# Fourier mixing and a gated feed-forward on one core: block 1 of sequence 0 takes the ordinary norm path, and four DMA issues move to later slots

## The chip, the cores and the metric

The kernel runs on one core of one Trainium2 chip. The metric is device time in microseconds (us). Before the change the median of 3 runs is 859.65 us (859.43 to 859.67).

## What is computed

Eight sequences `x[b]` of 3008 rows and 256 columns are filtered in the frequency domain along the rows, and the result goes row by row through an RMS norm and a gated feed-forward with 1536 hidden columns:

```python
X = np.fft.rfft(x, axis=1)
y = np.fft.irfft(X * (filt_r + 1j * filt_i)[None], n=x.shape[1], axis=1)
rows = y.reshape(8 * 3008, 256)
xn = rows / np.sqrt(np.mean(rows * rows, axis=-1, keepdims=True) + 1e-06) * rms_g
g = xn @ w_gate
out = (g * (1 / (1 + np.exp(-g))) * (xn @ w_val)) @ w_out
```

## The kernel before

**The Fourier part of a sequence.** 3008 is 47 x 64, and the transforms are matrix products in two steps. A sequence is read in four chunks (`x_load`, L174, issued on POOL's DMA queue into four buffers; 384 KB as it lands). `a_unit` (L213) does the first step on TensorE (PE), with one matmul of 128x512 (L204), and ACT or DVE copies the result from the matmul banks to the tile t1 (L195 or L197); there are 12 such units in a sequence, three for each chunk. When a chunk is done, `z_store` (L216) writes it to a buffer in DRAM on SP's DMA queue, and `t2_load` (L226) reads it back in another order once all four stores have landed. `b_unit` (L243, matmuls in L248) does the second step and multiplies by the filter; `bi_unit` (L287) and then `n_unit` (L313) do the inverse steps, with DMA transpositions (`yt_load` L280, `t4_load` L303) between them. The first steps of sequence 0 have functions of their own and fill the first 43 us.

**The norm and the feed-forward.** A sequence is handled in 6 blocks of 512 rows. For each block a normed and transposed tile xn is made, and then 12 items use it, one for each 128 hidden columns (`gv`, L539): four matmuls of 128x512 (L553, into the banks pg and pv), the silu on ACT (L557) and the product on DVE (L558). Two items later `down` (L561) multiplies by the last weights (L578). There are 8 x 6 x 12 = 576 items, and PE runs them in order. The banks pg and pv exist twice each, so item i needs those of item i - 2 to be read.

The ordinary way to xn, used for all blocks but two, is `n_unit` (one matmul of 128x512 on PE in L321, a copy to the tile y on ACT, twice), `sq_unit` (L325: squares with sums on ACT, two instructions for each half), `stat_unit` (L332: two small instructions on POOL, L337 and L339), `xt_unit` (L342: the scaling on POOL, L347) and `tr_unit` (L352: a DMA transposition on SP's queue, L356). Block 0 of sequence 0 has `first_norm` (L445). Block 1 of sequence 0 has four functions of its own before the change, which make xn without a DMA: `n_first` (L480) makes y already transposed, by 8 matmuls of 128x128 (L489), with two squares and two copies on ACT; `q_unit` (L498) sums the squares by 8 matmuls with a column of ones (L503) and takes the power on POOL (L509); `scale_split` (L512) makes two halves of the scale on DVE; `scale_apply` (L519) spreads it over the partitions by 8 matmuls of 128x128 (L525), and two multiplications on DVE (L530) write xn.

**What sets the order.** The order of issue is planned by hand in *slots*, one for each of the 576 items. `at(slot, fn, ...)` (L749) puts a function into a slot; in the last loop (L879 on) each item issues its `gv`, then what its slot holds, then `down` of the item two before. A slot is only a place in each engine's program: an engine goes on to its next instruction as soon as the semaphores that this one waits for are there, whatever slot the other engines are in. `fit` (L756) looks for the first slot from a wished one on in which the shared matmul banks ("M" and "B") are free and the load on ACT ("A") and DVE ("V") stays under a bound; `norm_plan` (L775), `a_plan` (L784) and `b_plan` (L799) use it. `norm_plan(b, m, slots, r)` puts the two `n_unit`s at the slots given (or later), their `sq_unit`s one slot behind each, and `stat_unit`, `xt_unit` and `tr_unit` so many slots behind the second as `r` says. Before the change, block 1's four functions stand at slots 3, 5, 7 and 9, and the load tables are set by hand for them (L829 to L831). Block 1's first item is item 12.

The chunks of sequence 2 are read at the slots that `XAT[2]` gives, or two slots behind the last `a_unit` of the chunk whose buffer they take, if that is later. The four stores of sequence 1 stand at slot 2 and, in `a_plan`, one slot behind the third unit of each chunk.

Of the kernel before, what the change touches and what calls it, by code (L numbers as in the profile page):

```python
# [10 lines left out]
FP32 = mybir.dt.float32  # L11
FP16 = mybir.dt.float16
AXT = mybir.ActivationFunctionType
ALU = mybir.AluOpType
# [6 lines left out]
P = 128  # L21
D = 256
B = 8
# [9 lines left out]
Y_SCALE = N * S_INV_B * S_INV_A  # L33
XC = 6
# [67 lines left out]
def kernel(  # L102
# [11 lines left out]
    nc = tc.nc  # L114
# [17 lines left out]
    xtp = ctx.enter_context(tc.tile_pool(name="xtp", bufs=2))  # L132
    up = ctx.enter_context(tc.tile_pool(name="up", bufs=2))
    xnp = ctx.enter_context(tc.tile_pool(name="xnp", bufs=4))
    hp = ctx.enter_context(tc.tile_pool(name="hp", bufs=4))
    op = ctx.enter_context(tc.tile_pool(name="op", bufs=2))
# [4 lines left out]
    psB = ctx.enter_context(tc.tile_pool(name="psB", bufs=1, space=bass.MemoryType.PSUM))  # L141

    tab = glob.tile([P, 5 * P], FP16)
    wa, wai, ident = (tab[:, ts(i, P)] for i in range(3))
# [13 lines left out]
    ones = glob.tile([P, 1], FP16)  # L158
    epsb = glob.tile([P, 1], FP32)
    warm = glob.tile([P, 4], FP32)  # L160
    mhalf = glob.tile([P, 4], FP32)
    seen = glob.tile([P, 4], FP16)

    st = {b: {"x": {}, "t1": {}, "t2": {}, "s": {}, "yt": {}, "t4": {}, "y": {}, "sq": {},
              "u": {}, "xn": {}} for b in range(B)}
# [4 lines left out]
    def y_tile():  # L170
        t = stg.tile([P, 2, 4, 256], FP32, tag="stg", name="y")
        return t.rearrange("p a b c -> p (a b c)")[:, 0:1024].rearrange("p (a e) -> p a e", a=2)
# [16 lines left out]
    def bank(i, name):  # L189
        pool, tag = ((psM, "mx"), (psG, "pg"), (psV, "pv"), (psB, "mb"), (psO, "po0"))[i]  # L190
        return pool.tile([P, 512], FP32, tag=tag, name=name)

    def copy(eng, out, in_, scale=None):
        if eng == "A":
            nc.scalar.activation(out=out, in_=in_, func=AXT.Copy, **({} if scale is None else {"scale": scale}))  # L195
        elif scale is None:
            nc.vector.tensor_copy(out=out, in_=in_)  # L197
        else:
            nc.vector.tensor_scalar(out=out, in0=in_, scalar1=scale, scalar2=None, op0=ALU.mult)
# [277 lines left out]
        nc.scalar.activation(out=warm, in_=mhalf, func=AXT.Silu)  # L477
        st[0]["xn"][0] = xn

    def n_first(m):  # L480
        y = y_tile()
        sq = xtp.tile([P, 4, D], FP16, tag="xt", name="sq").rearrange("p (a e) d -> p a (e d)", a=2)
        psn = [bank((0, 3)[h], "psn") for h in range(2)]
        for h in range(2):
            for q in (2 * h, 2 * h + 1):
                n1p = 4 * m + q
                src = st[0]["t4"][n1p // XC][:, n1p % XC]
                for dh in range(2):
                    nc.tensor.matmul(psn[h][:, ts(2 * (q % 2) + dh, P)], src[:, ds(dh * P, P)], wai,  # L489
                                     start=True, stop=True)  # L490
        for h in range(2):
            nc.scalar.activation(out=sq[:, h, :], in_=psn[h], func=AXT.Square)
        for h in range(2):
            copy("A", y[:, h, :], psn[h])
        st[0]["sq"][m] = sq
        st[0]["y"][m] = y

    def q_unit(m):  # L498
        sq = st[0]["sq"].pop(m)
        ps = psB.tile([P, 4], FP32, tag="mb", name="psq")  # L500
        for q in range(4):
            for dh in range(2):
                nc.tensor.matmul(ps[:, q:q + 1], sq[:, q // 2, ts(2 * (q % 2) + dh, P)], ones,  # L503
                                 start=(dh == 0), stop=(dh == 1))
        u = up.tile([P, 4], FP32, tag="u", name="u")
        rho = up.tile([P, 4], FP32, tag="rho", name="rho")
        nc.vector.tensor_scalar(out=u, in0=ps, scalar1=1.0 / D, scalar2=1e-6 * Y_SCALE * Y_SCALE,
                                op0=ALU.mult, op1=ALU.add)
        nc.gpsimd.tensor_tensor(out=rho, in0=u, in1=mhalf, op=ALU.pow)  # L509
        st[0]["u"][m] = rho  # L510

    def scale_split(m):  # L512
        rho = st[0]["u"].pop(m)
        hl = up.tile([P, 2, 4], FP16, tag="hl", name="hl")
        nc.vector.tensor_copy(out=hl[:, 0, :], in_=rho)
        nc.vector.tensor_tensor(out=hl[:, 1, :], in0=rho, in1=hl[:, 0, :], op=ALU.subtract)
        st[0]["u"][m] = hl

    def scale_apply(m, bk):  # L519
        hl = st[0]["u"].pop(m)  # L520
        y = st[0]["y"].pop(m)
        ps = bank(bk, "psr")
        for q in range(4):
            for e in range(2):
                nc.tensor.matmul(ps[:, ts(q, P)], hl[:, e, q:q + 1].to_broadcast([P, P]), ident,  # L525
                                 start=(e == 0), stop=(e == 1))
        xn = xnp.tile([P, 4, 2, P], FP16, tag="xn", name="xn")
        pv = ps.rearrange("p (q t) -> p q t", q=4)
        for h in range(2):
            nc.vector.tensor_tensor(out=xn[:, 2 * h:2 * h + 2],  # L530
                                    in0=pv[:, 2 * h:2 * h + 2].unsqueeze(2).to_broadcast([P, 2, 2, P]),
                                    in1=y[:, h, :].rearrange("p (q e t) -> p q e t", q=2, e=2), op=ALU.mult)
        st[0]["xn"][m] = xn

    LAST = (B - 1, 5)
    hh_of = {}
    po_of = {}
# [92 lines left out]
    with tc.manual_schedule():  # L630
# [48 lines left out]
        todo = [(i, f, dh) for i in range(2) for f in range(2) for dh in range(2)][:7] + [(2, 0, 0)]  # L679
# [58 lines left out]
        a_out(1, 2, "V", ahead[0])  # L738

        items = [(b, m, jt) for b in range(B) for m in range(6) for jt in range(JT)]  # L740
        plan, late = {}, {}
        front = (sq_unit, s_part, add_unit)
        load = {r: [0.0] * (len(items) + 99) for r in "MBAV"}
        room = {"A": 0.8, "V": 0.7}
# [2 lines left out]
            load["V"][i] = 0.68  # L747

        def at(slot, fn, *a):  # L749
            todo = (late if fn == q_unit else plan).setdefault(slot, [])  # L750
            if fn in front:
                todo.insert(0, (fn, a))
            else:
                todo.append((fn, a))
# [20 lines left out]
        def norm_plan(b, m, slots, r):  # L775
            for i in range(2):
                s = fit(slots[i], ("M", 0, 1), ("A", 0, 0.6), ("A", 1, 0.82))
                at(s, n_unit, b, m, i)
                at(s + 1, sq_unit, b, m, i)
            for d, fn in zip(r, (stat_unit, xt_unit, tr_unit)):  # L780
                at(s + d, fn, b, m)
            assert s + r[-1] + 1 < 72 * b + 12 * m

        def a_plan(b, slots):  # L784
            for i in range(4 * (b == 1), 12):
                opts = []
                for k in "MB":
                    opts.append((k, "A", ((k, 0, 1), ("A", 0, 0.6))))
                    opts.append((k, "V", ((k, 0, 1), (k, 1, 1), ("V", 0, 0.68))))
                k, e, need = min(opts, key=lambda o: fit(slots[i], *o[2], keep=False))  # L790
                s = fit(slots[i], *need)
                at(s, a_unit, b, i, e, 0 if k == 'M' else 3)
                if i % 3 == 2:
                    at(s + 1, z_store, b, i // 3)
                    if b + 1 < B:
                        at(max(s + 2, XAT.get(b + 1, (0,) * 4)[i // 3]), x_load, b + 1, i // 3)
            return s + 1
# [20 lines left out]
                        at(last, bi_unit, b, u)  # L818
            return last

        XAT = {2: (6, 8, 11, 29), 3: (47, 51, 79, 88), 4: (112, 122, 132, 142)}
        at(0, a_out, 1, 3, "A", ahead[1])
        at(2, z_store, 1, 0)
        at(XAT[2][0], x_load, 2, 0)
        at(3, n_first, 1)
        at(5, q_unit, 1)
        at(7, scale_split, 1)
        at(9, scale_apply, 1, 3)
        load["M"][3] = load["M"][4] = 1  # L829
        load["B"][3] = load["B"][4] = load["B"][5] = load["B"][9] = load["B"][10] = 1  # L830
        load["A"][3] = load["A"][4] = 1.2  # L831
        for m, n_at in ((2, 12), (3, 20), (4, 31), (5, 42)):
            norm_plan(0, m, (n_at, n_at + 2), (2, 3, 6))
        for b in range(1, B):
            t = (b - 1) * 72
# [43 lines left out]
        for i in range(len(items) + 4):  # L879
            for fn, a in early.pop(i, ()):  # L880
                fn(*a)
            if i < len(items):
                gv(*items[i])
            for fn, a in plan.pop(i, ()):
                fn(*a)
            if 2 <= i < len(items) + 2:
                b, m, jt = items[i - 2]
                if jt == 1 and i > JT:
                    down(b, m, 0)
                if jt or i < JT:  # L890
                    down(b, m, jt)
                if items[i - 2][2] == JT - 1:
                    stores[i + 1] = items[i - 2][:2]
            for fn, a in late.pop(i, ()):
                fn(*a)
            if i in stores:
                o_store(*stores[i])
        assert not plan and not late and not early


# [28 lines left out]
```

## Time and profile before

| what | value |
|---|---|
| median of 3 runs | 859.65 us (859.43 to 859.67) |
| the profiled execution | 859.65 us |
| its span, first to last instruction | 857.9 us |
| around the span | 1.75 us |
| mean granted clock of PE | 1.000 |
| PE busy from 43 to 150 us | 107.0 of 107 us |
| DMA engines from 43 to 150 us | 82% busy, 164 GB/s |
| x loads (384 KB), issue to landing | 6.1 us (median of 31) |
| z stores, issue to landing | 2.7 us (median of 28) |
| transpositions to xn, issue to landing | 3.0 / 3.6 / 8.1 us (least, median, most of 46) |

A line of a timeline gives the start and the length of an instruction (or of several alike, with their number) in us, the engine, the line of the kernel, the operation, and what is written from what. Matmuls overlap, so the cost of one on PE is read from start to start. SPq is the DMA queue that SP issues to; a DMA's length there is the time that the issue takes, and its landing is told apart. POOL, with the name of a DMA operation, is such an issue by POOL. A page of waits names who waited, for whom, and how long. The granted clock is the share of TensorE's full clock that the chip gave.

### The profile page before, as it was taken

The page shows a single profiled execution, that of the slowest core. Times are in us where ns is not written, and L with a number is a line of the kernel's source. Part 1 is how long each engine was busy: PE and PEld are TensorE (multiplying, and loading weights), DVE is VectorE, ACT ScalarE, POOL GpSimd, SP SyncE. Part 2 cuts the span into 40 slices and gives each one's busy share as a digit, 9 for nine tenths or more (in the row PEclk, how much of TensorE's full clock was granted, in tenths as well). Part 3 has the DMA queues.
Part 4 walks back from the last instruction along what each step waited for, and adds up shares of the span by engine and source line. Part 5 has one row for each costly group of instructions (what it writes and reads, how often), then busy time and mean ns, then how long its engine had stood idle before and what let it go on. Part 6 is the DMA issues. An engine that isn't in the chain of part 4 may idle for free.

```text
span 857.9 us, 17015 instructions
## 1 busy us (share of the span) xinstructions
PE 849.2 (99%) x6139; PEld 532.5 (62%) x6139; DVE 557.2 (65%) x926; ACT 612.5 (71%) x1338; POOL 298.1 (35%) x346
## 2 busy tenths in 40 slices
PE   8999999999999999999999999999999999999997
PEld 6766666666666666666666666666666666665655
DVE  5857755776666666666666676767666665555554
ACT  4987887786687757887578865887567765777444
POOL 5725732543154413443044430444123430132000
PEclk9999999999999999999999999999999999999999
DMA  9995878756975566746747658434574431521101
GB/s 282 273 206 126 152 169 168 148 123 137 186 138 140 108 142 114 158 117 129 152 122 115 120 108 185 105 81 113 122 126 93 98 69 42 123 56 50 63 25 50
DMA packets 198237, 107.98 MB, mean 126 GB/s; under 512 B 158566, under 2 KB 182520, under 8 KB 198152
## 3 DMA queue, kind: packets, MB, share of 16 engines
q1 hardware_dynamic: 189464, 85.52, 44.9%
q0 software_dynamic: 8544, 21.24, 12.9%
q8 instruction: 48, 0.79, 0.4%
q14 instruction: 37, 0.30, 0.1%
q10 hardware_dynamic: 144, 0.13, 0.0%
HBM read 45.78 MB, written 35.65 MB: 95 GB/s over the span
## 4 chain that ended last, share of the span: by engine, by line
PE 97%; DMA 1%; DVE 0%; ACT 0%; POOL 0%; issue 0%; DVEq 0%; POOLq 0%
PE po L578 29%; PE pg L553 28%; PE pv L553 28%; PE psb L248 3%; PE psi L292 3%; PE psn L321 2%; PE psa L204 2%; DMA fs<-in_filt_i_dram 1%; PE psy L425 1%; PE psf L396 1%; PE pst L374 0%; POOL xc L186 0%; DVE s L238 0%; ACT ff L195 0%; ACT sq L455 0%
## 5 line engine op out<-in xcount | busy, mean ns | idle before, releaser
L558 DVE TENSOR_TENSOR hh<-pv,sg 128x512 f16<-128x512 f32 (+1 forms) x577 | 391.6, 679 | 283.4 <-ACT sg L557 220.5
L557 ACT ACTIVATE sg<-pg 128x512 f16<-128x512 f32 (+1 forms) x577 | 337.5, 585 | 215.2 <-PE pg L553 211.4
L553 PE MATMUL pg<-xn,wg 128*128 128x512 f16 (+2 forms) x1156 | 337.9, 374 | 0.0
L553 PE MATMUL pv<-xn,wv 128*128 128x512 f16 (+2 forms) x1156 | 337.8, 374 | 0.0
L578 PE MATMUL po<-wo,hh 128*128 128x256 f16 x2256 | 332.7, 272 | 0.0
L578 PEld LDWEIGHTS <-hh 128*128 128x128 f16 x2256 | 213.4, 98 | 105.2
L275 POOL TENSOR_TENSOR ss<-s,s 128x384 f16<-128x384 f16 x112 | 102.0, 912 | 267.4 <-DVE s L241 239.8
L553 PEld LDWEIGHTS <-wv 128*128 128x128 f16 x1156 | 113.0, 98 | 130.6 <-issue 0.2
L553 PEld LDWEIGHTS <-wg 128*128 128x128 f16 x1156 | 111.5, 98 | 16.9 <-issue 0.2
L347 POOL TENSOR_TENSOR xt<-y,rho 128x1024 f16<-128x1024 f32 (+1 forms) x46 | 85.4, 1857 | 2.9
L329 ACT ACTIVATE junk<-y 128x256 f16<-128x256 f32 x180 | 74.3, 413 | 2.8
L238 DVE TENSOR_TENSOR s<-psb,ff 128x384 f16<-128x384 f32 x124 | 67.8, 548 | 0.7 <-ACT ff L195 0.6
L241 DVE TENSOR_TENSOR s<-psb,ff 128x384 f16<-128x384 f32 x124 | 67.7, 547 | 0.0
L195 ACT ACTIVATE uu<-psi 128x384 f16<-128x384 f32 (+1 forms) x127 | 61.8, 487 | 1.1
L195 ACT ACTIVATE y<-psn 128x512 f32<-128x512 f32 (+1 forms) x95 | 55.7, 588 | 4.2
L292 PEld LDWEIGHTS <-yt 96*128 96x128 f16 x512 | 35.5, 97 | 26.2 <-issue 0.2
L339 POOL TENSOR_TENSOR rho<-u,mhalf 128x4 f32<-128x4 f32 (+1 forms) x46 | 46.5, 1011 | 3.8
L337 POOL TENSOR_SCALAR u<-ss 128x4 f32<-128x4 f32 (+1 forms) x46 | 8.9, 194 | 106.4 <-ACT junk L329 105.4
L195 ACT ACTIVATE t<-psa 128x512 f16<-128x512 f32 x70 | 41.4, 595 | 2.8 <-PE psa L204 1.4
L292 PE MATMUL psi<-wi,yt 96*128 96x96 f16 x512 | 42.9, 205 | 0.0
L248 PE MATMUL psb<-wb,t 96*128 96x96 f16 x480 | 40.0, 206 | 0.0
L248 PEld LDWEIGHTS <-t 96*128 96x128 f16 x480 | 29.3, 97 | 10.7 <-issue 0.2
(102 smaller groups left out, 364.2 us busy)
## 6 DMA issues: line engine op xcount, KB each, us to landing
out_dram<-o SPq DMA_DIRECT2D x40, 512.0 KB, 3.5
xc<-in_x_dram POOLq DMA_DIRECT2D x31, 384.0 KB, 6.1
z_tmp<-t SPq DMA_DIRECT2D x28, 384.0 KB, 2.7
t<-z_tmp SPq DMA_DIRECT2D x28, 384.0 KB, 6.0
out_dram<-o SPq DMA_DIRECT2D x7, 384.0 KB, 2.7
fs<-in_filt_i_dram POOLq DMA_DIRECT2D x3, 512.0 KB, 10.8
fs<-in_filt_r_dram POOLq DMA_DIRECT2D x3, 512.0 KB, 11.3
ws<-in_moe_w_gate_dram POOLq DMA_DIRECT2D x3, 512.0 KB, 10.0
```

Source lines behind the costliest of these rows:

```text
L195: nc.scalar.activation(out=out, in_=in_, func=AXT.Copy, **({} if scale is None else {"scale": scale}))
L238: eng.tensor_tensor(out=o, in0=ps, in1=f1, op=ALU.mult)
L241: eng.tensor_tensor(out=o, in0=ps[:, :, ::-1, :], in1=f2, op=ALU.mult)
L248: nc.tensor.matmul(ps[:, ts(k, KR)], st[b]["t2"][kk // KC][:, kk % KC, ds(dh * P, P)], wb[0:KR, kk, :], start=True, stop=True)
L275: nc.gpsimd.tensor_tensor(out=ss3[g % 3][:, :, dh, 0:KR], in0=s[0], in1=s[1], op=ALU.add)
L292: nc.tensor.matmul(ps[:, k, :], yt[0:KR, k, dh, :], wi[0:KR, 4 * g + k, :], start=True, stop=True)
L329: nc.scalar.activation(out=junk, in_=y[:, i, ts(u, D)], func=AXT.Square, accum_out=ss[:, 2 * i + u:2 * i + u + 1])
L347: nc.gpsimd.tensor_tensor(out=xt[:, 0:n, :], in0=y.rearrange("p a (u d) -> p (a u) d", u=2)[:, 0:n, :], in1=rho[:, 0:n].unsqueeze(2).to_br ...
L553: nc.tensor.matmul(ps[:, (r0 - q0) * P:(r1 - q0) * P], wt[:, dt_, ts(jt, P)], xn[:, r0:r1, dt_, :], start=(dt_ == 0), stop=(dt_ == 1))
L557: nc.scalar.activation(out=sg[:, c], in_=pg[:, 0:w], func=AXT.Silu)
L558: nc.vector.tensor_tensor(out=hh[:, c], in0=pv[:, 0:w], in1=sg[:, c], op=ALU.mult)
L578: nc.tensor.matmul(po[q - 1][:, 0, :] if own else po[q // 2][:, q % 2, :], hh_of[(b, m, j)][:, ts(q, P)], wo[:, j, :], start=(j == 0 and ( ...
```

## The change

Block 1 of sequence 0 goes the ordinary way: `norm_plan(0, 1, (2, 3), (2, 3, 5))` takes the place of its four functions, which are removed, with what the planner held for them (the dictionary `late`, and the loads set by hand). Three reads of sequence 2 (its chunks 0, 1 and 2) are put at slots 12, 13 and 15 in place of 6, 8 and 11. The store of chunk 1 of sequence 1 is put at slot 9; before, it stood one slot behind its third unit.

In the issue order of each engine this gives: on PE, one L321 matmul at slot 2 and one at slot 3 in place of the groups L489, L503 and L525, and one L204 matmul moves from slot 6 to slot 4, its copy from ACT to DVE. On ACT, two copies and four squares with sums in place of two squares and two copies. On DVE, the five small and large instructions of L507, L515, L516 and L530 go. On POOL, L337, L339 and L347 stand where L509 stood, and the three loads L186 come directly behind L347, as they came directly behind L509. On SP, one transposition L356 stands between the first and the second store L218. All other instructions keep their order.

```diff
-    def n_first(m):
...
-    def q_unit(m):
...
-    def scale_split(m):
...
-    def scale_apply(m, bk):
...
-        plan, late = {}, {}
+        plan = {}
...
         def at(slot, fn, *a):
-            todo = (late if fn == q_unit else plan).setdefault(slot, [])
+            todo = plan.setdefault(slot, [])
...
                 if i % 3 == 2:
-                    at(s + 1, z_store, b, i // 3)
+                    at(9 if (b, i) == (1, 5) else s + 1, z_store, b, i // 3)
...
-        XAT = {2: (6, 8, 11, 29), 3: (47, 51, 79, 88), 4: (112, 122, 132, 142)}
+        XAT = {2: (12, 13, 15, 29), 3: (47, 51, 79, 88), 4: (112, 122, 132, 142)}
         at(0, a_out, 1, 3, "A", ahead[1])
         at(2, z_store, 1, 0)
         at(XAT[2][0], x_load, 2, 0)
-        at(3, n_first, 1)
-        at(5, q_unit, 1)
-        at(7, scale_split, 1)
-        at(9, scale_apply, 1, 3)
-        load["M"][3] = load["M"][4] = 1
-        load["B"][3] = load["B"][4] = load["B"][5] = load["B"][9] = load["B"][10] = 1
-        load["A"][3] = load["A"][4] = 1.2
+        norm_plan(0, 1, (2, 3), (2, 3, 5))
```

More of the change, by code (lines that the diff above doesn't have):

```diff
@@ L478, in first_norm @@
         st[0]["xn"][0] = xn
-    def n_first(m):
[L481 to L496, printed above, removed]
@@ L498, in q_unit @@
-    def q_unit(m):
[L499 to L510, printed above, removed]
@@ L512, in scale_split @@
-    def scale_split(m):
[L513 to L517, printed above, removed]
-    def scale_apply(m, bk):
[L520 to L533, printed above, removed]
@@ L893 @@
                     stores[i + 1] = items[i - 2][:2]
-            for fn, a in late.pop(i, ()):
-                fn(*a)
             if i in stores:
                 o_store(*stores[i])
-        assert not plan and not late and not early
+        assert not plan and not early
 _INS = ['x', 'filt_r', 'filt_i', 'moe_w_gate', 'moe_w_val', 'moe_w_out', 'moe_rms_g']
```

## The prediction

> **What bounds the kernel now.** I read the shares of each engine, then the chain that ended last, then what TensorE (PE) waited for, all of the profile before.
>
> ```profile
> PE 849.2 (99%) x6139; PEld 532.5 (62%) x6139; DVE 557.2 (65%) x926; ACT 612.5 (71%) x1338; POOL 298.1 (35%) x346
> ...
> PE 97%; DMA 1%; DVE 0%; ACT 0%; POOL 0%; issue 0%; DVEq 0%; POOLq 0%
> ```
>
> PE is busy for 99% of the span and is 97% of the chain. Asked for PE's waits from 43 us on (where the feed-forward part begins) to the end, the profile lists none. So any PE work removed there shortens the run by its own length, and any wait that the change gives PE lengthens it by its own length, since no gap is left to take it up.
>
> The timeline of PE around the change (start, length, engine, line, operation):
>
> ```profile
> 47.30 0.61 PE L489 MATMUL psn<-tab,t 128*128 128x128 f16 x8
> 47.74 0.60 PE L578 MATMUL po<-wo,hh 128*128 128x256 f16 x4
> ...
> 51.00 0.34 PE L503 MATMUL psq<-ones,sq 128*128 128x1 f16 x8
> 51.20 0.59 PE L553 MATMUL pg<-xn,wg 128*128 128x512 f16 x2
> ...
> 56.83 0.61 PE L525 MATMUL psr<-tab,hl 128*128 128x128 f16 x8
> 57.27 0.38 PE L204 MATMUL psa<-xc,tab 128*128 128x512 f16 x1
> ...
> 60.95 0.59 PE L553 MATMUL pg<-xn,wg 128*128 128x512 f16 x2
> ...
> 61.82 0.38 PE L321 MATMUL psn<-t,tab 128*128 128x512 f16 x1
> 62.03 0.60 PE L578 MATMUL po<-wo,hh 128*128 128x256 f16 x4
> ```
>
> From start to start, the three groups of block 1's own norm cost 0.44, 0.20 and 0.44 us; an ordinary norm matmul (L321) costs 0.21. The matmul at 60.95 is the first that reads block 1's normed tile: this is the deadline of everything below.
>
> **The change, part by part.**
>
> *PE.* Removed: 0.44 + 0.20 + 0.44 = 1.08 us. Added: two L321 matmuls, 0.43. Sum **-0.65 us**, on the path. One forward-transform matmul (L204) moves from slot 6 to slot 4: no change in sum. The deadline becomes 60.95 - 0.65 = 60.30.
>
> *ACT and DVE.* ACT loses two squares and two copies of 128x512 (about 0.5 us each) and gets two copies and four squares with sums (two of them take 0.95 by the rows at 66.45 to 67.42), 0.9 us more. The silu of slot 4 then ends near 50.0 instead of 50.3, the multiplication behind it near 50.8; PE reuses their banks at 51.2 and 51.6. So nothing waits. DVE loses 1.75 us and gets a copy of 0.69. Both are hidden by the slack in the two engines (71% and 65%).
>
> *POOL and the transposition.* This is the new path to the deadline. Its pattern is block 2's in the same trace (ACT, POOL, and the DMA queue of SP):
>
> ```profile
> 67.33 0.19 ACT L329 ACTIVATION_READ_ACCUMULATOR junk<-y 128x1 f32 x1
> ...
> 67.61 0.19 POOL L337 TENSOR_SCALAR u<-ss 128x4 f32<-128x4 f32 x1 [11.04 <-ACT junk L329]
> 67.90 1.04 POOL L339 TENSOR_TENSOR rho<-u,mhalf 128x4 f32<-128x4 f32 x1
> 69.02 1.89 POOL L347 TENSOR_TENSOR xt<-y,rho 128x1024 f16<-128x1024 f32 x1
> ...
> 70.94 1.26 SPq L356 DMA_TRANSPOSE xn<-xt  x1
> ```
>
> From the last sum (67.52) to the transposition's issue it takes 3.4 us. For block 1: the two norm matmuls start at 46.0 and 47.5 (their tiles landed by 46.06, where POOL's L733 was released), the second copy ends near 48.5, and ACT then does two squares, a silu and two squares: last sum near 50.95, issue near **54.3**. A transposition that has the DMA engines for itself lands 3.0 us (that at 363.40) to 3.6 us (that at 70.94) after its issue: 57.9, 2.4 us ahead of the deadline. So far the change would be a gain of 0.65.
>
> *The x loads.* In POOL's program the three loads of sequence 2 now stand directly behind the xt multiplication. A slot orders only what one engine issues. POOL issues a load without waiting for the transposition, which SP issues when the same multiplication ends. So the loads, issued at 52.83, 53.4 and 55.98 before, go at 54.25, 54.9 and 55.8: in the same moment as the transposition, not behind its landing. That moment occurs later in this trace, with one load:
>
> ```profile
> 387.29 0.64 POOL L186 DMA_DIRECT2D xc<-in_x_dram  x1
> ...
> 387.37 1.23 SPq L356 DMA_TRANSPOSE xn<-xt  x1
> ```
>
> The load comes 0.08 us before the transposition, as at 265.63 and 265.72. Both of these transpositions landed 5.9 us after issue. DMA queues from 390.1 to 391.1 us (packets, MB, share of 16 engines; q0 is POOL's, q1 SP's):
>
> ```profile
> q1 hardware_dynamic: 62, 0.02, 12.0%
> ...
> q0 software_dynamic: 63, 0.19, 99.6%
> ```
>
> One packet of the load (3 KB) goes for one of the transposition (256 bytes). A load is 384 KB, 128 packets; a transposition is 256 KB, 1024 packets. So it creeps until the load is through, and most of its packets go behind it. Two more loads are 2 x 128 / 63 = 4.1 us more; 250 more of its packets slip through meanwhile, which saves some 0.3 at the end. Landing: 5.9 + 4.1 - 0.3 = 9.7 us after issue, at **64.0**. PE waits 64.0 + 0.05 - 60.30 = **3.75 us**. The extremes for this landing are 3.0 us (no wait) and 5.9 + 4.1 + 1.2 (a second load that starts as slowly as the one of 116.92, behind which packets were scarce for 1.2 us): a wait of 0 to 5.2. I take 9.7, since both rows nearest to it have the same issue order.
>
> [...]
>
> *The store of sequence 1* (second of four) goes behind the transposition in SP's queue: 53.10 becomes 55.6. What waits behind it are the third (its data are ready at 56.1) and the fourth store (61.34). They share SP's DMA queue with the transposition, so now their packets follow it, from about 63.3; three stores take 3 us of packets, so the last lands near 67.4. Their reader, the load L228, was issued at 66.06, landed 4.7 us later, and PE took it at 71.14: 0.38 us to spare. With PE 3.75 later, that load goes behind the output store of block 0 near 69, as far ahead of PE as before. Cost nothing, because PE's own wait covers it; without that wait it is 0 to 1.5 us (rival B).
>
> *Sum.* The profiled execution took 859.65 us (span 857.9, 1.75 around it), which is also the median. 859.65 - 0.65 + 3.75 = 862.75, so **862.8 us**. Own range 861.0 (only two loads in front: a landing after 7.9) to 864.0 (the slow start).
>
> **Rivals.**
>
> *B: the transposition gets through beside the loads, not slower.* It decides at one point, a landing less than 6.0 us after issue. For it: 5.9 with one load would just do; SP's issue could win over POOL's, or a turn hold several of its packets. Against it: the one-for-one turns, and three loads. Then PE doesn't wait at the deadline, but the transposition and the later loads push the fourth store back by up to 1.3 us, and L248's first weights come up to 1.5 us late: 859.65 - 0.65 + 0 to 1.5, that is 859.0 to 860.5; I say 860.0. Chance 0.16.
>
> *C: the wait also slows PE's clock.* At the span's start, after idleness, ten matmuls of 128x512 that cost 0.22 each later took 4.01 us, 1.7 too long:
>
> ```profile
> 1.45 4.01 PE L433 MATMUL pf<-ss 128*128 128x512 f16 x10 [1.45 <-DVE epsb L632]
> ```
>
> If PE's wait brings this back, 862.8 + 1.7 = 864.5. Against it: no idle time inside the span is as long, so none shows it, and waits to 0.64 us did nothing. [...] Chance 0.12.
>
> *D: the removed PE work is worth more than its length,* or the loads are held elsewhere and nothing is late: 859.0 or less. Chance 0.04; nothing in the profile speaks for more than 0.65.
>
> **How the numbers follow.** Forecast 0.68, C 0.12, B 0.16, D 0.04. A measurement of this kernel tells 0.2% (1.7 us) from no change. Above 861.4: the forecast and C but for a tail, 0.79. Within: B, D's greater part and that tail, 0.19. Faster: 0.02. For the range the forecast and C alone leave out a little over 0.2, so it reaches into B: 860.2 to 865.0.
>
> **What would show it.** In the profile after: a PE wait of some 3.7 us at the first pg matmul of block 1 near 60.3, put down to the DMA of xn; L186 and L356 issued within 0.2 us of each other near 54.3; that transposition landing 9 to 10 us after issue, and few of SP's packets until the loads are through. PE's sum there is right if the pg matmul is ready at 60.3. No PE wait at that matmul and one at L248 would be B; pf-like slow matmuls behind the wait, or a granted clock below 1, would be C. I am wrong if the x loads start later than the transposition lands.

## The result, and the profile after

The changed kernel takes 863.46 us (median of 6 runs, 862.65 to 865.56) against 859.61 us (6 runs, 859.43 to 859.78): a ratio of 1.005, with a 95% interval of 1.0035 to 1.0064. It is slower by about 0.45%. The runs of the kernel before lie within 0.35 us, those of the changed one within 2.9, and the granted clock sorts them: 862.65, 862.71 and 862.87 at a mean of 1.000, 864.06 at 0.998, 865.37 and 865.56 at 0.995. The profiled execution is that of 862.71 us (span 860.9).

From L498 on, a line of the changed kernel has a number lower by 55: its `gv` matmuls are L498, its `down` is L523. Shares of the engines, and the chain that ended last:

```profile
PE 849.6 (99%) x6117; PEld 532.1 (62%) x6117; DVE 555.9 (65%) x922; ACT 612.5 (71%) x1343; POOL 299.7 (35%) x348
...
PE 95%; DMA 2%; POOL 1%; ACT 1%; DVE 0%; issue 0%; POOLq 0%
```

PE's share of the chain fell from 97% to 95%, and POOL, ACT and more of the DMA now stand in it. The waits of PE from 40 to 160 us name the place (who waited, for whom, then us in total, times, and the longest):

```profile
PE pg L498 <- DMA xn<-xt: 3.5, 1, 3.5
PE psr L473 <- DVE rho L468: 0.2, 1, 0.2
```

The second is at 42.4 us, ahead of block 0's first item, and stands in the kernel before too. So from 43 us on there is one wait, and the DMA that ends it is the transposition of block 1's normed tile. On PE's timeline the two new norm matmuls, and the first matmul of block 1 (brackets at the end of a line tell how long the engine was idle before it, and what released it):

```profile
45.90 0.38 PE L321 MATMUL psn<-t,tab 128*128 128x512 f16 x1
...
47.42 0.38 PE L321 MATMUL psn<-t,tab 128*128 128x512 f16 x1
...
63.88 0.59 PE L498 MATMUL pg<-xn,wg 128*128 128x512 f16 x2 [3.52 <-DMA xn<-xt]
```

POOL's timeline, with the path to the transposition and, directly behind it, the three loads:

```profile
50.88 0.18 POOL L337 TENSOR_SCALAR u<-ss 128x4 f32<-128x4 f32 x1 [3.44 <-ACT junk L329]
51.16 1.05 POOL L339 TENSOR_TENSOR rho<-u,mhalf 128x4 f32<-128x4 f32 x1
52.28 1.89 POOL L347 TENSOR_TENSOR xt<-y,rho 128x1024 f16<-128x1024 f32 x1
54.12 1.28 POOL L186 DMA_DIRECT2D xc<-in_x_dram  x2
55.67 0.59 POOL L186 DMA_DIRECT2D xc<-in_x_dram  x1 [0.27 <-PE psa L204]
```

And SP's queue:

```profile
54.20 1.23 SPq L356 DMA_TRANSPOSE xn<-xt  x1
55.54 5.36 SPq L218 DMA_DIRECT2D z_tmp<-t  x3
68.06 0.68 SPq L546 DMA_DIRECT2D out_dram<-o  x1
68.98 2.22 SPq L228 DMA_DIRECT2D t<-z_tmp  x3
```

The first load is issued 0.08 us before the transposition. What the two queues moved from 57.25 to 58.25 us (packets, MB, share of the 16 engines):

```profile
q0 software_dynamic: 62, 0.19, 96.3%
q1 hardware_dynamic: 63, 0.02, 12.2%
```

In that 1 us, 62 packets of the loads and 63 of the transposition went, one for one, as at 390 us in the kernel before (63 and 62). The transposition, issued at 54.20, is there when PE goes on at 63.88, 9.7 us later.

### The profile page after: what moved, and what is told of

It is laid out like the page before. It is cut to its first block, busy times and chain, and to the rows that moved or that the text cites. A ratio compares the mean times of both kernels' runs of the same rounds, so it can differ in the third digit from the quotient of the medians.

```text
span 860.9 us, 16980 instructions
## 1 busy us (share of the span) xinstructions
PE 849.6 (99%) x6117; PEld 532.1 (62%) x6117; DVE 555.9 (65%) x922; ACT 612.5 (71%) x1343; POOL 299.7 (35%) x348
## 4 chain that ended last, share of the span: by engine, by line
PE 95%; DMA 2%; POOL 1%; ACT 1%; DVE 0%; issue 0%; POOLq 0%
PE po L523 28%; PE pg L498 28%; PE pv L498 28%; PE psb L248 3%; PE psi L292 3%; PE psn L321 2%; PE psa L204 2%; DMA xn<-xt 1%; DMA fs<-in_filt_i_dram 1%; PE psy L425 1%; PE psf L396 1%; PE pst L374 0%; POOL xc L186 0%; POOL xt L347 0%; DVE s L238 0%
## 5 line engine op out<-in xcount | busy, mean ns | idle before, releaser
L503 DVE TENSOR_TENSOR hh<-pv,sg 128x512 f16<-128x512 f32 (+1 forms) x577 | 391.2, 678 | 287.8 <-ACT sg L502 220.0
L498 PE MATMUL pg<-xn,wg 128*128 128x512 f16 (+2 forms) x1156 | 337.9, 374 | 3.5 <-DMA xn<-xt 3.5
L498 PE MATMUL pv<-xn,wv 128*128 128x512 f16 (+2 forms) x1156 | 337.8, 374 | 0.0
L523 PE MATMUL po<-wo,hh 128*128 128x256 f16 x2256 | 332.6, 272 | 0.0
L523 PEld LDWEIGHTS <-hh 128*128 128x128 f16 x2256 | 213.5, 98 | 105.5
L498 PEld LDWEIGHTS <-wv 128*128 128x128 f16 x1156 | 113.0, 98 | 130.7 <-issue 0.2
L498 PEld LDWEIGHTS <-wg 128*128 128x128 f16 x1156 | 111.6, 98 | 20.5 <-issue 3.9
L347 POOL TENSOR_TENSOR xt<-y,rho 128x1024 f16<-128x1024 f32 (+1 forms) x47 | 87.2, 1856 | 2.9
L339 POOL TENSOR_TENSOR rho<-u,mhalf 128x4 f32<-128x4 f32 (+1 forms) x47 | 47.5, 1011 | 3.9
L337 POOL TENSOR_SCALAR u<-ss 128x4 f32<-128x4 f32 (+1 forms) x47 | 9.1, 193 | 113.0 <-ACT junk L329 111.8
L248 PE MATMUL psb<-wb,t 96*128 96x96 f16 x480 | 40.0, 206 | 0.0
L248 PEld LDWEIGHTS <-t 96*128 96x128 f16 x480 | 29.3, 97 | 10.7 <-issue 0.2
```

What stands on the lines that cost most here:

```text
L248: nc.tensor.matmul(ps[:, ts(k, KR)], st[b]["t2"][kk // KC][:, kk % KC, ds(dh * P, P)], wb[0:KR, kk, :], start=True, stop=True)
L347: nc.gpsimd.tensor_tensor(out=xt[:, 0:n, :], in0=y.rearrange("p a (u d) -> p (a u) d", u=2)[:, 0:n, :], in1=rho[:, 0:n].unsqueeze(2).to_br ...
L498: nc.tensor.matmul(ps[:, (r0 - q0) * P:(r1 - q0) * P], wt[:, dt_, ts(jt, P)], xn[:, r0:r1, dt_, :], start=(dt_ == 0), stop=(dt_ == 1))
L503: nc.vector.tensor_tensor(out=hh[:, c], in0=pv[:, 0:w], in1=sg[:, c], op=ALU.mult)
L523: nc.tensor.matmul(po[q - 1][:, 0, :] if own else po[q // 2][:, q % 2, :], hh_of[(b, m, j)][:, ts(q, P)], wo[:, j, :], start=(j == 0 and ( ...
```

## The experiments

Ten kernels ran, all but one of them edits of the changed kernel. E8 and E9 build on e1. "Before" is the kernel before, run beside them on the same chip: 859.75 us beside e1, e3, e4 and e7, 859.68 beside e0, e2, e6 and e8, 859.72 beside e5 and e9.

| kernel | median us (runs) | range | ratio to before (95%) | granted clock of the runs |
|---|---|---|---|---|
| e0 changed kernel again | 864.35 (5) | 862.83 to 865.45 | 1.0053 (1.004 to 1.0066) | 1.000, 3 x 0.998, 0.995 |
| e1 loads behind the landing | 860.95 (11) | 860.56 to 861.80 | 1.0013 (1.0005 to 1.0022) | 0.999 to 1.000 |
| e4 one load beside | 863.44 (4) | 862.06 to 865.23 | 1.0046 (1.003 to 1.0061) | 2 x 1.000, 0.998, 0.995 |
| e5 two loads beside | 862.75 (4) | 862.17 to 863.28 | 1.0035 (1.0021 to 1.0049) | 2 x 1.000, 2 x 0.998 |
| e2 loads at the old slots | 863.77 (5) | 863.36 to 865.96 | 1.0048 (1.0034 to 1.0061) | 4 x 0.998, 0.996 |
| e6 store at the old slot | 864.49 (4) | 862.88 to 864.68 | 1.0052 (1.0038 to 1.0065) | 1.000, 3 x 0.998 |
| e3 PE busy in the wait | 863.22 (5) | 862.74 to 864.35 | 1.0042 (1.003 to 1.0055) | 0.999 to 1.000 |
| e7 wait made longer | 866.67 (5) | 866.10 to 866.79 | 1.0078 (1.0066 to 1.0091) | 4 x 0.996, 0.998 |
| e8 first load early | 860.45 (11) | 859.66 to 861.26 | 1.0008 (0.9999 to 1.0017) | 0.999 to 1.000 |
| e9 two loads early | 859.47 (11) | 859.06 to 860.56 | 0.9999 (0.999 to 1.0008) | 0.999 to 1.000 |

**Theory and rivals.** The theory is the prediction's: POOL issues the x loads in the same moment as SP issues the transposition, they share the DMA engines packet by packet, and PE waits for what comes of it. Its rivals: the new path through ACT, POOL and the DMA is too long by itself; the stores behind the transposition are what costs; and, for the spread, that either the clock or the landing differs from run to run.

**e1: the loads wait for the landing.**

```diff
+        def see(m):
+            nc.gpsimd.tensor_copy(out=seen, in_=st[0]["xn"][m][:, 0, 0, 0:4])
...
         norm_plan(0, 1, (2, 3), (2, 3, 5))
+        at(11, see, 1)
```

> The changed kernel, with one small POOL copy that reads block 1's normed tile put ahead of the three loads of sequence 2, so that POOL issues them only when the transposition has landed. Theory (the loads beside the transposition hold it up): it lands 3.0 to 3.6 us after its issue at 54.2, near 57.5; PE does not wait at the first matmul of block 1; the loads go out near 57.6 in place of 54.1; 859.0 to 859.8 us, the upper end if the last store of sequence 1 now comes a little late. Rival 1 (the new path itself, ACT to POOL to DMA, is too long): PE still waits some 3.5 us there, 862.5 or more. Rival 2 (the stores behind the transposition are what costs): the wait at the first matmul of block 1 goes, but one of 2 us or more comes up at L248.

POOL's timeline of e1, the small copy that is released by the landing:

```profile
57.56 0.19 POOL L767 COPY seen<-xn 128x4 f16<-128x4 f16 x1 [3.12 <-DMA xn<-xt]
```

The transposition was issued at 54.46 and landed 3.1 us later; PE's wait at block 1's first matmul is gone. So the path by itself is short enough, and the loads made it long. But the time fell to 860.95 only, over 1 us above the 859.0 to 859.8 expected, because another wait came up, by PE's waits from 43 to 120 us:

```profile
PE psb L248 <- DMA t<-z_tmp: 1.6, 1, 1.6
```

Among SP's own waits (60 to 72 us) is that of the load which reads the stores back:

```profile
SPq L228 <- DMA z_tmp<-t: 3.2, 1, 3.2
```

And the last store was issued, by SP's timeline, at 60.84:

```profile
60.84 0.32 SPq L218 DMA_DIRECT2D z_tmp<-t  x1
```

That store landed 7.8 us after its issue. In the stretch from 61.0 to 64.4 us only POOL's queue moved anything, by the page of DMA queues of that window, which has no line for SP's:

```profile
q0 software_dynamic: 244, 0.66, 110.0%
```

So the loads, now issued from 58.05 on, stand in front of the store. This is the second wait that rival B priced, with 1.6 us in place of 0 to 1.5.

**e4 and e5: one or two loads beside the transposition.** The same edit, with the copy behind the first or the second load: `at(12, see, 1)` and `at(14, see, 1)` in place of slot 11.

> As e1, but one load stays beside the transposition and two wait for its landing. Theory (one packet of the load for one of the transposition): it lands 5.9 us after issue as the two of the kernel before with one load beside them, near 60.1; PE waits 0 to 0.4 us at the first matmul of block 1; 859.0 to 860.5 us. If the number of loads does not matter once one is there: landing 9.6 us after issue as in the changed kernel, 862.7.

> As e4, but two loads stay beside the transposition and one waits for its landing. By one packet for one, the landing grows by about 2 us for each load: with 0, 1 and 3 loads beside it 3.1, 6.1 and 9.6 us were seen, so 7.5 to 8.5 us are expected here, and a wait of 1.5 to 2.5 us at block 1's first matmul. The third load then stands beside the last store of sequence 1, and a wait at L248 of 0 to 2 us may come on top: 860.5 to 863.0 us. If instead the transposition is held until everything that POOL has issued is through, whatever its amount, the landing is the same; if the number of loads did not matter, 9.6 us.

POOL's copy in e4, where the transposition was issued at 55.04:

```profile
61.12 0.18 POOL L767 COPY seen<-xn 128x4 f16<-128x4 f16 x1 [5.50 <-DMA xn<-xt]
```

And in e5, where it was issued at 54.12:

```profile
62.84 0.18 POOL L767 COPY seen<-xn 128x4 f16<-128x4 f16 x1 [7.52 <-DMA xn<-xt]
```

With 0, 1, 2 and 3 loads beside it, the transposition lands 3.1, 6.1, 8.7 and 9.7 us after its issue. The number of loads does it. The 8.7 of e5 is a little above the 7.5 to 8.5 expected; its waits are 2.5 and 0.5 us, and its runs at full clock took 862.17 and 862.23.

The time of e4 missed its expectation by 3 us. PE doesn't wait at block 1's first matmul, as expected, but at L248:

```profile
PE psb L248 <- DMA t<-z_tmp: 3.2, 1, 3.2
```

Here the last store is not held up: issued at 61.42, it landed 3.0 us later. The load that reads the stores back is, by SP's timeline issued from 66.19 on:

```profile
66.19 4.09 SPq L228 DMA_DIRECT2D t<-z_tmp  x3
```

Its three parts landed 8.6 to 9.2 us after their issue (3.8 to 6.0 in e1). The two x loads held back were still moving, and SP's queue moved next to nothing, by the page of DMA queues from 63.5 to 67.5 us:

```profile
q0 software_dynamic: 233, 0.67, 101.1%
...
q1 hardware_dynamic: 2, 0.00, 0.4%
```

**e2: the loads at their old slots.**

```diff
-        XAT = {2: (12, 13, 15, 29), 3: (47, 51, 79, 88), 4: (112, 122, 132, 142)}
+        XAT = {2: (6, 8, 11, 29), 3: (47, 51, 79, 88), 4: (112, 122, 132, 142)}
```

> The changed kernel with the x loads of sequence 2 left at their old slots (6, 8, 11); POOL then issues the first of them ahead of block 1's scaling, and the other two directly behind it. Theory: the same three loads still stand beside the transposition, only the first starts some 2 us earlier and the scaling 0.6 us later; the loads are through about 1 us earlier than in the changed kernel; PE waits 2 to 3.5 us, 861 to 863 us. So the new slots of the loads do nothing by themselves. Rival (the new slots are what makes the change slow): no wait for the transposition, 859 to 860 us. Other rival (the new slots do help, as they are meant to): 864 us or more.

POOL issued the loads at 52.24, 54.73 and 55.74 and SP the transposition at 54.83. The transposition landed 10.2 us after its issue, and PE waited 4.6 us in the profiled execution (of 865.96 us). I had expected the loads to be through earlier, and a wait of 2 to 3.5; that failed. What holds is that the slots make little difference: 863.77 against 864.35 for e0, with overlapping ranges. The new slots moved the loads by 1.9 us at most, and not behind the landing.

**e6: the store at its old slot.**

```diff
-                    at(9 if (b, i) == (1, 5) else s + 1, z_store, b, i // 3)
+                    at(s + 1, z_store, b, i // 3)
```

> The changed kernel with the second store of sequence 1 back at its old slot, ahead of the transposition in SP's queue; the loads stay beside. Theory: the store's packets go first and take turns with the loads', so the transposition starts creeping later and lands 0.5 to 1.5 us later than in the changed kernel: 863.2 to 864.2 us in runs whose clock stays at 1.000. Rival (the store is what costs in the changed kernel): 860 us or less.

SP issued the store ahead of the transposition. PE's wait was 3.5 us as in the changed kernel, and the one run at full clock took 862.88, as the changed kernel's (862.65 to 862.87). The expected extra 0.5 to 1.5 us did not come, and the rival's gain did not either: the store's place costs nothing that these runs show. The profiled execution is one of the three at 0.998 (864.68 us); what it shows of the clock follows below.

**e3 and e7: is it the clock?** In e3 PE has 14 matmuls that nothing reads ahead of block 1's first item, 3.0 us of work inside the wait. In e7 the scaling of block 1 is done twice on POOL, so that PE waits longer.

```diff
+        at(11, fill, 14, 3)
```

```diff
-        nc.gpsimd.tensor_tensor(out=xt[:, 0:n, :],
...
+        for _ in range(2 if (b, m) == (0, 1) else 1):
+            nc.gpsimd.tensor_tensor(out=xt[:, 0:n, :],
...
```

> The changed kernel, with 14 matmuls of 128x512 that nothing reads put on PE just ahead of block 1's first item; 14 x 0.216 = 3.0 us of work that fits in the wait of 3.5. Theory (half of the changed kernel's runs are 1.4 to 2.9 us longer than 862.7 because the wait brings down PE's granted clock for a while): with PE busy through the wait, all runs come out near 862.7, their spread is under 0.6 us, and the granted clock is 1.000 in each. Rival (the spread comes from the transposition's landing, which differs from run to run): the spread of 2.9 us stays, the longest runs still near 865.5.

> The changed kernel, with block 1's scaling on POOL done twice (the same result): 1.9 us more on the path to the transposition, and the loads behind it shift with it. Theory: PE's wait grows from 3.5 to 5.4 us, and by the clock theory it now brings the granted clock down in every run: 862.7 + 1.9 + 2.7 = 867.3 us, spread under 1 us, granted clock about 0.995. Without an effect of the clock: 864.6 us, granted clock 1.000.

In e7 the wait is 5.4 us, and the matmuls behind it are slow. PE's timeline of e7, first matmuls of block 1:

```profile
65.68 1.01 PE L499 MATMUL pg<-xn,wg 128*128 128x512 f16 x2 [5.39 <-DMA xn<-xt]
66.49 1.06 PE L499 MATMUL pv<-xn,wv 128*128 128x512 f16 x2
```

The busy times of e7's engines in the window from 65.6 to 69.3 us (PE, PEld, DVE, ACT, POOL, then the granted clock, the DMA share and GB/s):

```profile
65.60:69.30 3.70, 3.62 (x11) 1.61 (x11) 0.69 (x1) 1.19 (x2) 0.00 (x0) 0.52 0.70 271
```

The pair of matmuls takes 0.81 us from start to start there and 0.43 in the changed kernel at full clock; the clock is 0.52 in that window. The work from 65.68 to 69.32 takes 1.95 us elsewhere, so the slow stretch costs 1.7. The whole run agrees: 862.7 + 1.9 + 1.7 = 866.3, and 866.10 to 866.79 were measured. My expectation of 867.3 had put 2.7 for the clock and was 0.6 too high.

A wait of 3.5 us can do the same. E6's profiled execution has that wait, and its first matmuls of block 1 are slow too:

```profile
64.25 0.87 PE L498 MATMUL pg<-xn,wg 128*128 128x512 f16 x2 [3.50 <-DMA xn<-xt]
```

Its busy times from 64.43 to 67.84 us, with a clock of 0.50; and those of e7 from 62.34 to 69.16:

```profile
64.43:67.84 3.41, 3.41 (x11) 1.52 (x10) 0.69 (x1) 1.20 (x2) 0.00 (x0) 0.50 0.40 152
```

```profile
62.34:69.16 6.82, 3.48 (x11) 1.57 (x11) 0.69 (x1) 1.19 (x2) 0.00 (x0) 0.50 0.88 258
```

Work that takes 3.41 us at a clock of 0.50 is 1.7 us longer than at 1.00 (3.41 x 0.50). In the changed kernel's own profile, with the same wait of 3.5 us, the clock stays at 1.00.

In e3, with PE kept busy, no run is above 864.4 and the clock is 0.999 or 1.000 in all; but 1.6 us of spread remain at full clock, which I had put under 0.6. So the clock makes the longest runs. What makes the rest is not shown: a landing that differs from run to run would do it, but the profiled execution of e3 is one of its short ones, and e9, with no wait of PE in its profile, has a spread of 1.5 us too.

**e0: the changed kernel again.**

> The changed kernel again, with nothing altered, for the spread of its times beside the granted clock. Clock theory: the runs above 865 show a granted clock of 0.995 or 0.996, those near 862.7 show 1.000 (or the 0.999 that the kernel before shows now and then); median 862.7 to 865. Rival: no relation between time and granted clock.

Over both sets, four runs at 1.000 lie between 862.65 and 862.87, four at 0.998 between 864.06 and 864.36, and three at 0.995 between 865.37 and 865.56. The relation is clear.

**e8 and e9: loads early.** E1's copy stays. In e8 the first load goes behind the last one of sequence 1; in e9 the second one too, as soon as its buffer is read.

```diff
-        XAT = {2: (12, 13, 15, 29), 3: (47, 51, 79, 88), 4: (112, 122, 132, 142)}
+        XAT = {2: (1, 13, 15, 29), 3: (47, 51, 79, 88), 4: (112, 122, 132, 142)}
```

```diff
-                        at(max(s + 2, XAT.get(b + 1, (0,) * 4)[i // 3]), x_load, b + 1, i // 3)
+                        at(s if (b, i) == (1, 5) else max(s + 2, XAT.get(b + 1, (0,) * 4)[i // 3]), x_load, b + 1, i // 3)
```

> As e1 (loads behind the landing of the transposition), but the first of the three goes out early, directly behind the last load of sequence 1, and two wait for the landing. Theory: e1's 1.6 us at L248 comes from 6 us of loads ahead of and beside the last store of sequence 1; with 4 us of them the store lands 2 us earlier, the wait at L248 goes or is under 0.5, and the transposition (beside the tail of one load at most) still lands before 60.3: 859.0 to 859.6 us, the level of the kernel before or a little under it. Rival (the store is slow for another reason): 860.9 as e1. If the early load holds the transposition up, a wait at block 1's first matmul instead: 860 to 861.

> As e8, but the second load too goes out early (on POOL between the power and the scaling of block 1), and only the third waits for the transposition's landing. In e1 and e8 the last store of sequence 1, issued near 60.8 us, moved its first packet only when the loads were nearly through (64.6 and 64.8 us). With a single load behind the landing the loads are through near 63.5, the store lands near 65.5, and the wait at L248 goes. The early loads are through near 58, so the transposition, issued at 54.8, lands near 59.8, just ahead of its deadline of 60.3. Theory: no wait of over 0.3 us at either place, 859.0 to 859.6 us. Rival (a store that starts late whatever the loads): 860.4 as e8. If the early loads last longer than thought: a wait at block 1's first matmul of up to 2 us, 860 to 861.

E8 missed its expectation: the last store, issued at 60.74, again landed 7.8 us later, with two loads in front in place of three, and PE waited 1.6 us at L248. E9 came out in the time expected, but not quite by the course expected: the last store, issued at 60.61, landed 6.4 us later, at 67.0 in place of 65.5, which is still early enough. POOL's copy in e9 (transposition issued at 54.78):

```profile
59.73 0.18 POOL L767 COPY seen<-xn 128x4 f16<-128x4 f16 x1 [4.98 <-DMA xn<-xt]
```

On SP's queue the stores are read back 1.5 us earlier than in e1 and e8 (68.75 and 68.72):

```profile
67.17 1.50 SPq L228 DMA_DIRECT2D t<-z_tmp  x3
```

PE waited nowhere after 43 us, and the span is 857.3 us in place of 857.9: the 0.65 us of removed work, kept at last. Over 11 runs this can't be told from the kernel before (ratio 0.9999, 0.999 to 1.0008).

## Why the prediction was right, and where it was off

**The removed PE work, -0.65 us: right.** In e1, where nothing waits on the way, PE needs 17.10 us from block 0's first matmul (43.36) to block 1's (60.46); the kernel before needs 17.75 (43.20 to 60.95).

**ACT and DVE hidden: right.** From 43 us on the changed kernel has no PE wait but the one at the deadline.

**The path to the transposition: right.** Issue at 54.3 was forecast, 54.20 measured; alone it lands 3.1 us later (e1), within the 3.0 to 3.6 of the forecast.

**The loads in the same moment: right,** at 54.12 and 55.67 for the first and the third. E1 shows that they are the cause, e2 that their slots are not, e4 and e5 that the cost grows with their number.

**The landing, 9.7 us after issue: right in sum, not in its course.** I took 5.9 us with one load and had each of the other two add 2 us, with most of the transposition's packets behind the last load. One load gave 6.1, the second added 2.6, the third 1.0. In the changed kernel the second load began to move only 0.6 us after the first was through, and 510 packets of the transposition used that gap (58.4 to 59.0 us); 776 of its 1024 went between 58.0 and 59.5. What was left crept on one for one (47 packets of each queue from 59.5 to 60.5) and was through before the third load, which landed at 66.0. So the third load cost little, the second more than I thought, and that the sum came out at 9.7 is luck. (The slow start that I gave as the other end, 864.0, is 864.2 by its own terms.) The wait came out as 63.88 - (43.10 + 17.10) = 3.68 us from start to start, against 3.75.

**The store behind the transposition: right for this kernel** (no wait at L248; e6), **too small without the cover.** I had priced 0 to 1.5 us; e1 and e8 show 1.6 by way of the last store, e4 3.2 by way of the load that reads the stores back. The failed term is the store's delay of 1.3 us: in e1, beside POOL's loads, it moved nothing from 61.0 to 64.4 us and landed 7.8 us after its issue.

**The clock, rival C: its chance was too low.** 862.8 us was forecast at full clock, and 862.65 to 862.87 were measured there. But I gave 0.12 to the slow clock, since no wait of this trace was as long, and 7 of 11 runs of the changed kernel have it. The chance was my estimate, and the step that failed is to read waits of up to 0.64 us, which did nothing, as a sign against one of 3.75: in e7 the clock fell 2.05 us into a wait of 5.39, in e2 some 2.1 us into one of 4.64 (last section). The price of 1.7 us is what the rows of e7 and e6 show, and the runs at 0.998 are 1.5 us above those at full clock. Those at 0.995 are 2.7 above. No such run of this kernel has a profile, so how much of that is a slower clock and how much a later landing stays open; in e2's profiled execution, at 0.996, both are there, a wait of 4.6 us in place of 3.5 and slow work that costs 2.1. The median of 863.46 lies between the groups, so that it is near the forecast, which is the time of a run at full clock, is in part luck.

**Rival B: refuted.** PE waits at block 1's first matmul, and one packet goes for one (62 and 63 in the rows above). **Rival D: refuted** by the 0.65 us of e1.

## What to carry to other kernels

A place in an engine's program did not order one engine's DMA behind another's: with the loads at slots 12, 13 and 15, POOL issued the first at 54.12 us and SP the transposition at 54.20. What did was a wait for something that the landing releases: in e1 POOL's small copy came at 57.56, with the landing, and the loads from 58.05 on. When loads are moved away from one transfer with a deadline, the next transfer in line must be looked at too: held back, they cost 1.6 us by way of the last store (e1, e8), or 3.2 by way of the load behind it (e4), and only two loads earlier and one later cost nothing (e9). And a single wait on PE cost more than its length: behind one of 3.5 us in e6, work at a clock of 0.50 took 1.7 us more.

## What the runs showed that was not expected

A transfer that SP issued while POOL's loads were moving started late in three runs. In e1 the store issued at 60.84 moved nothing from 61.0 to 64.4 us and landed after 7.8 us, in e8 that of 60.74 moved nothing from 61.0 to 64.6 and landed after 7.8 too, and in e4 it was the load L228, landed after 8.6 to 9.2; the median of such stores in the kernel before is 2.7 us. The cause was not tried.

The granted clock, as the mean of a run, was below 0.999 in some runs with a wait of PE and not in others. By the wait in the kernel's profiled execution: with 5.4 us (e7) and 4.6 (e2) in all ten runs, with 3.5 us (the changed kernel, e0, e6) in 10 of 15, with 2.5 to 3.2 us (e5, e4) in 4 of 8, with 1.6 us or none (e1, e8, e9) in none. Three profiles show the fall itself. In e6 the clock was 0.50 for 3.41 us, from 0.18 us after the wait's end; in e7 for 6.82 us, from 2.05 us into the wait; in e2 for some 6.9 us, from some 2.1 us into it. (The last two figures are estimates from e2's clock in three windows: 0.75 from 60 to 65 us, 0.50 to 69, 0.97 to 75.) In the profiled executions of the changed kernel, e0, e4 and e5, waits of 3.5, 3.5, 3.2 and 2.5 us left the mean clock of the run at 1.000. So the same wait of 3.5 us cost nothing more in two of these profiles and 1.7 us more in the third. What decides between them is not shown.
